# Linear attention followed by a normalised two-layer block: row statistics without bn_stats, more transposes by DMA, and a new order of the same work

## The chip, the cores and the metric

The kernel runs on one core of a Trainium2 chip. A core has five engines with a queue each: TensorE (PE: matmuls, and weight loads shown as PEld), VectorE (DVE), ScalarE (ACT), GpSimd (POOL) and SyncE (SP), which here only issues transfers. Sixteen DMA engines carry the transfers. The metric is the time of one execution on the device in microseconds (us). The kernel before took 157.92 us (median of 3 runs, 157.91 to 160.95).

## The reference

The inputs are `r`, `k`, `v` (4 batches, 8 heads, 768 time steps, head dimension 48), a decay `w` and a bonus `u` per head and channel. The first half is a linear attention with a decaying state, the second half normalises each row of 384 channels and sends it through 384 to 1536 to 384 with a ReLU:

```python
for t in range(S):
    cur = einsum('bhd,bhe->bhde', u[None] * kt, vt)
    y[:, :, t] = einsum('bhd,bhde->bhe', rt, state + cur)
    state = w[None, :, :, None] * state + einsum('bhd,bhe->bhde', kt, vt)
x = y.transpose(0, 2, 1, 3).reshape(B, S, H * D)
mu, var = mean(x, -1), mean((x - mu) ** 2, -1)
xn = (x - mu) / sqrt(var + 1e-06) * g_ln
out = x + maximum(xn @ w_ch1, 0.0) @ w_ch2
```

Inputs and output are float32. The matmul operands in the kernel are bfloat16.

## The kernel before, in words

**Tiles.** The 768 time steps of a batch are cut into 6 chunks of 128, which makes 24 chunks; chunk i of the attention is tile i (128 rows by 384 channels) of the second half. Tiles are taken through the two-layer block in 18 groups, of one tile at first and at the end and of two in the middle (tiles 8 to 19).

**Steps of a chunk.** LK, LR and LV (lines 315 to 322) load k, r and v of a chunk on SP's queue, 192 KB each; in DRAM a row of a head is 48 floats. SK and SR multiply k and r by powers of the decay into bfloat16 tiles `sck` and `scr`. TR (line 333) turns `scr` and `sck` on TensorE, four transposes each, into PSUM; TC, TCr and TCk copy them to `trs` in SBUF. For the chunks in `K_BY_DMA` (18 to 23) k is turned instead by TKD, a DMA transpose that SP issues (line 475), and TR turns r alone. Q multiplies the two halves of `trs`. AT (line 352) forms the 128 by 128 scores of 8 heads, AM masks them on VectorE into `A`, S (line 383) makes the state's update and the bonus, CC copies the bonus out, ZU and ZD update the state `Z`, VB multiplies v by the bonus on GpSimd, Y (line 425) sums the attention in PSUM and X (line 444) adds VB's part: this is `x`.

**Steps of a tile.** ST and AG (lines 447 to 452) take mean and variance of a row with bn_stats and bn_aggr. XN writes mean minus x in bfloat16 (the sign is in the weights, which SW scales by minus g_ln at the start). RS (line 464) forms one over the standard deviation on GpSimd. LT turns the tile on TensorE, three transposes, and XT copies it to `xT`. UP (line 488) does the first layer, in three steps of 12 matmuls for a group of one tile and six steps of 6 wider matmuls for a pair, each into a PSUM tile of 512 columns (two such buffers, `hp`); RL is the ReLU that empties it into `hT`. DN (line 517) does the second layer in three steps of four matmuls into one PSUM tile `o`. OT multiplies by RS and adds x, STO stores the tile.

**Order.** The order of all this is written out in the string `PLAN`: every entry names a step, a chunk (or group and part) and an engine (v, s, g; "-" where the step has only one). Each engine's queue gets its instructions in the order of PLAN and works through them in that order; semaphores set by the framework make an instruction wait for what it reads and for buffers to come free. `SLOTS` gives the number of buffers of each kind: 10 for the loaded k, r and v, 3 for `sck`, `scr` and `trs`, 2 for `q`. All loads, all stores and all DMA transposes stand in the one queue of SP, in the order of PLAN, and each transfer there also waits for the completion of the one eight places ahead. DU steps are matmuls on a zero tile in the first microseconds.

Of the kernel before, what the change touches and what calls it, by code (L numbers as in the profile page):

```python
# [15 lines left out]
K_BY_DMA = [18, 19, 20, 21, 22, 23]  # L16
SLOTS = {'kf': 10, 'rf': 10, 'vf': 10, 'sck': 3, 'scr': 3, 'vv': 4, 'trs': 3, 'q': 2, 'A': 2, 'cc': 4, 'Z': 3, 'ZS': 2, 'Vb': 3, 'x': 13, 'xn': 3, 'xT': 4, 'hT': 4, 'ot': 3}
PLAN = """
MW,0,v WF,0,- TL,0,s MI,0,g MP,0,v WU,13,- MM,0,g LN,0,s LK,0,- ROWSI,0,s WBM,0,- LV,1,-
LR,0,- FK,0,s CV,1,v FR,0,s SK,0,v LK,1,- SR,0,g LR,1,- SK,1,v DU,18,- TR,0,- UW,0,g  # L20
WL,0,s LK,2,- SR,1,g TCk,0,s LR,2,- TCr,0,s SK,2,g Q,0,v DU,22,- TR,1,- LV,0,- AT,0,-
TCk,1,s SR,2,v LG,0,- LW1,2,- TCr,1,s AMa,0,v CV,0,g UGC,0,s AMb,0,v DU,13,- TR,2,- S,0,-
Q,1,v TC,2,s Y,0,- AT,1,- CC,0,v ZU,0,v LV,2,- AMa,1,v VB,0,g DU,3,- S,1,- SW,7,s
AMb,1,v LW1,1,- SW,8,s IW2,0,g X,0,v SW,6,s DU,13,- AT,2,- Q,2,v Y,1,- CV,2,g ST,0,v
AG,0,v LW1,0,- CC,1,s XN,0,s RS,0,g ZU,1,v SW,5,s SW,3,v DU,16,- LT,0,- VB,1,g XT,0,v
SW,4,s DU,6,- UP,2,- X,1,v S,2,- RL,2,s SW,2,g ST,1,v UP,1,- SW,0,s SW,1,v IW2,2,g
AG,1,v AM,2,v UP,0,- XN,1,s IW2,1,g LK,3,- LT,1,- RL,1,s CC,2,v XT,1,v LR,3,- DU,1,-
Y,2,- RL,0,s VB,2,g ZU,2,v UP,18,- SK,3,v LV,3,- DN,0,- SR,3,v RL,18,s UP,17,- X,2,v
TR,3,- CV,3,g ST,2,v RL,17,s UP,16,- RS,1,g TC,3,v AG,2,v RL,16,s Q,3,v AT,3,- XN,2,v
RS,2,g AM,3,v S,3,- LT,2,- DN,1,- XT,2,s CC,3,s UP,33,- ZU,3,v LK,4,- DN,2,- LV,6,-  # L30
VB,3,g UP,32,- OT,0,v Y,3,- SK,4,v LR,4,- DN,4,- RL,32,v RL,33,s DN,5,- CV,6,s LR,5,-
X,3,v SR,4,v DN,6,- LV,4,- ST,3,v TR,4,- SR,5,g UP,34,- OT,1,v LV,5,- TC,4,s AG,3,v
DN,8,- CV,4,v XN,3,g LK,5,- Q,4,v AT,4,- RL,34,s DN,9,- RS,3,g AM,4,v LK,7,- LT,3,-
S,4,- XT,3,s DN,10,- LK,6,- SK,5,v CC,4,s VB,4,g UP,48,- OT,2,v LR,10,- TR,5,- SK,7,v
UP,49,- SK,6,g ZU,4,v RL,48,s LR,6,- TC,5,v Y,4,- CV,5,s DN,12,- RL,49,v LR,12,- ZD,4,g
AT,5,- X,4,v DN,13,- AM,5,v LR,7,- SR,6,g UP,50,- LV,7,- ST,4,v TR,6,- RL,50,s Q,5,v
SR,7,g Y,5,- AG,4,v STO,1,- TC,6,v S,5,- XN,4,s DN,14,- STO,0,- CC,5,v CV,7,s Q,6,v
VB,5,g LT,4,- LV,11,- AT,6,- XT,4,v S,6,- OT,3,v UP,64,- LV,9,- X,5,v CC,6,s UP,66,-
RS,4,g ST,5,v RL,64,s LR,8,- TR,7,- AM,6,v RL,66,s UP,65,- SR,10,g CV,9,s LK,11,- DN,16,-
AG,5,v RL,65,s TC,7,v RS,5,g Y,6,- LR,9,- XN,5,s DN,17,- ZU,6,v VB,6,g Q,7,v LT,5,-  # L40
LK,8,- DN,18,- XT,5,s AT,7,- X,6,v LK,10,- UP,80,- ST,6,v S,7,- SR,8,v RL,80,s LR,14,-
UP,82,- SK,8,g AM,7,v UP,81,- RL,82,s LK,9,- TR,8,- CC,7,s AG,6,v OT,4,v RL,81,s RS,6,g
Y,7,- LK,14,- TC,8,v XN,6,s DN,20,- VB,7,g CV,11,s ZU,7,v LV,8,- LT,6,- DN,21,- Q,8,v
SR,9,g X,7,v XT,6,s AT,8,- LK,15,- SK,9,v DN,22,- CV,8,s UP,96,- ZD,7,g LV,13,- ST,7,v
AM,8,v TR,9,- RL,96,s SK,10,g STO,2,- S,8,- UP,97,- LR,11,- CC,8,s TC,9,v SR,12,g Y,8,-
OT,5,v RL,97,s TR,10,- STO,4,- Q,9,v AT,9,- VB,8,g LK,12,- TC,10,s AG,7,v UP,98,- ZU,8,v
AM,9,v ZD,8,g S,9,- LV,12,- XN,7,s DN,24,- CC,9,s LT,7,- Q,10,v SK,11,g LR,16,- DN,25,-
ZU,9,v RL,98,s X,8,v AT,10,- XT,7,s LV,15,- DN,26,- ZD,9,g ST,8,v UP,114,- AM,10,v LV,10,-
VB,9,g Y,9,- RL,114,s UP,113,- STO,3,- SR,11,g AG,8,v X,9,v XN,8,s LK,13,- UP,112,- CV,10,s
ST,9,v RS,7,g TR,11,- OT,6,v RL,112,s LR,17,- S,10,- AG,9,v TC,11,v RL,113,s SR,14,g Y,10,-  # L50
DN,28,- CC,10,s LR,15,- SK,13,v CV,12,s XN,9,s VB,10,g LT,8,- AT,11,- ZU,10,v LK,17,- DN,29,-
XT,8,s Q,11,v SK,12,g LT,9,- X,10,v DN,30,- LV,16,- XT,9,s AM,11,v S,11,- UP,130,- RS,8,g
LR,13,- UP,129,- CC,11,v OT,7,v RL,130,s ZD,10,g LK,21,- TR,12,- ST,10,v RL,129,s UP,132,- CV,13,v
VB,11,g TC,12,s SR,15,v LK,19,- UP,131,- RL,132,s Y,11,- STO,6,- SR,13,v AT,12,- RL,131,s LK,16,-
Q,12,v UP,128,- AG,10,v X,11,v XN,10,g S,12,- STO,5,- RL,128,s TR,13,- ST,11,v LK,22,- UP,133,-
CV,15,v SR,16,v SK,15,g DN,32,- TC,13,v RL,133,s LR,22,- DN,33,- AG,11,v AM,12,v XN,11,s Q,13,g
LR,21,- LT,10,- CC,12,s DN,34,- XT,10,s ZU,12,v Y,12,- LV,21,- SK,14,g LT,11,- OT,8,v AT,13,-
S,13,- XT,11,v DN,36,- LR,19,- VB,12,g AM,13,v TR,14,- CV,16,g LR,20,- UP,144,- CC,13,v X,12,v
TC,14,s RS,9,g DN,37,- ZU,13,v LV,14,- RL,144,s ST,12,v ZD,13,g UP,145,- STO,7,- UP,148,- RL,145,s
VB,13,g LV,20,- Q,14,v AT,14,- RL,148,s Y,13,- LK,18,- SK,16,v TR,15,- AG,12,v DN,38,- CV,14,v  # L60
TC,15,v LV,22,- UP,149,- OT,9,v XN,12,s TR,16,- LV,23,- Q,15,v RL,149,s DN,40,- X,13,v SR,19,g
LV,17,- ST,13,v UP,147,- TC,16,s AM,14,v UP,146,- LV,19,- RL,147,s LT,12,- CV,17,g S,14,- AG,13,v
RL,146,s XT,12,v AT,15,- LR,18,- CC,14,v Y,14,- XN,13,s SK,17,v DN,41,- ZU,14,v LR,23,- Q,16,v
LT,13,- DN,42,- VB,14,g AM,15,v XT,13,s LK,20,- S,15,- ZD,14,g UP,163,- OT,10,v STO,8,- UP,162,-
RL,163,s X,14,v SR,18,g DN,44,- SK,18,v SR,17,g UP,160,- ST,14,v STO,9,- AT,16,- RL,162,s CC,15,v
AG,14,v Y,15,- LK,23,- AM,16,v RL,160,s RS,10,g TR,17,- CV,19,s UP,164,- VB,15,g LV,18,- TC,17,v
UP,165,- RL,164,s SR,20,g ZU,15,v DN,45,- Q,17,v XN,14,s STO,10,- ZD,15,g TR,18,- S,16,- X,15,v
TCr,18,s DN,46,- ST,15,v UP,161,- AG,15,v OT,11,v Y,16,- RL,161,s SR,21,v XN,15,g AT,17,- TKD,18,-
CV,20,s LT,14,- CC,16,v DN,48,- XT,14,v RL,165,s VB,16,g LT,15,- DN,49,- XT,15,v Q,18,v RS,11,g
UP,180,- X,16,v STO,11,- ZU,16,v DN,50,- SK,19,g ST,16,v S,17,- TR,19,- OT,12,v UP,176,- RL,180,s  # L70
ZD,16,g AG,16,v CC,17,s DN,52,- AM,17,v VB,17,g UP,178,- RL,176,s TKD,19,- SK,20,g DN,53,- XN,16,v
RL,178,s Y,17,- STO,12,- CV,18,g UP,177,- TCr,19,s AT,18,- CV,21,s Q,19,g TR,20,- RL,177,s X,17,v
UP,181,- AM,18,v DN,54,- RL,181,s SR,22,g UP,179,- OT,13,v TKD,20,- SR,23,g AT,19,- ST,17,v RL,179,s
S,18,- DN,56,- TCr,20,v AG,17,v LT,16,- XN,17,s RS,12,g Y,18,- DN,57,- XT,16,v CC,18,s CV,22,s
ZU,18,v LT,17,- VB,18,g DN,58,- XT,17,v AM,19,v UP,197,- STO,13,- Q,20,g TR,21,- UP,192,- X,18,v
OT,14,v S,19,- AT,20,- RL,197,s SK,22,v DN,60,- TCr,21,s UP,195,- ST,18,v CC,19,s ZU,19,v DN,61,-
VB,19,g STO,14,- AM,20,v Y,19,- RL,195,s ZD,19,g S,20,- DN,62,- X,19,v RL,192,s TR,22,- CV,23,s
Y,20,- OT,15,v SK,21,g UP,194,- ST,19,v CC,20,s UP,193,- TCr,22,v RL,194,s TKD,22,- AG,19,v TR,23,-
VB,20,g RL,193,s UP,196,- AG,18,v XN,18,s TCr,23,v DN,64,- TKD,21,- XN,19,g X,20,v RL,196,s LT,18,-
DN,65,- RS,13,g XT,18,v STO,15,- AT,21,- SK,23,g ZU,20,v LT,19,- DN,66,- XT,19,v AM,21,v ZD,20,g  # L80
UP,212,- UP,209,- RL,212,s Q,21,g OT,16,v Y,21,- UP,208,- RL,209,s AT,22,- S,21,- Q,22,g AM,22,v
DN,68,- CC,21,s UP,213,- VB,21,g ZU,21,v RL,208,s DN,69,- ST,20,v RL,213,s STO,16,- ZD,21,g UP,211,-
AG,20,v S,22,- X,21,v RS,14,g RL,211,s DN,70,- ST,21,v TKD,23,- XN,20,s UP,210,- AG,21,v XN,21,v
RS,15,g LT,20,- Y,22,- OT,17,v AT,23,- CC,22,s XT,20,v RL,210,s DN,72,- VB,22,g ZU,22,v AM,23,v
UP,224,- ZD,22,g STO,17,- DN,73,- RL,224,v Q,23,g LT,21,- DN,74,- UP,225,- OT,18,v UP,226,- XT,21,v
RL,225,s X,22,v DN,76,- ST,22,v UP,241,- DN,77,- RL,241,s AG,22,v RL,226,v XN,22,g Y,23,- DN,78,-
STO,18,- RS,16,g UP,240,- OT,19,v LT,22,- S,23,- RL,240,s DN,80,- XT,22,s DN,81,- CC,23,s VB,23,g
UP,257,- DN,82,- RL,257,s X,23,v STO,19,- UP,256,- OT,20,v UP,242,- ST,23,v DN,84,- AG,23,v RL,242,s
XN,23,g DN,85,- RL,256,s RS,17,g LT,23,- DN,86,- XT,23,v UP,272,- OT,21,v UP,258,- STO,20,- DN,88,-
RL,258,s DN,89,- RL,272,s STO,21,- DN,90,- UP,273,- OT,22,v UP,274,- RL,273,s DN,92,- RL,274,s DN,93,-  # L90
STO,22,- DN,94,- OT,23,v STO,23,-
"""


@with_exitstack
def kernel(
    ctx: ExitStack,
    tc: tile.TileContext,
    r: bass.AP,
# [344 lines left out]
    def X(i, e):  # L444
        nc.vector.tensor_tensor(out=xx(i)[:], in0=psum["y", i][:, :C], in1=Vb(i)[:], op=ALU.add)  # L445
# [137 lines left out]
```

## Time and profile before

| | before |
|---|---|
| median of 3 runs | 157.92 us |
| profiled execution, its own time | 156.55 us |
| its span, first to last instruction | 154.4 us |
| PE busy | 146.4 us, 95% |
| DVE busy | 119.4 us, 77% |
| POOL busy | 95.7 us, 62% |
| ACT busy | 76.2 us, 49% |
| DMA transposes | 6, all of k |
| granted clock of TensorE | 0.996 |

The profiled execution was 1.37 us quicker than the median of the timed runs. Between its span and its own time lie 2.13 us. Busy time of PE is modelled and matmuls overlap, so two neighbouring rows of PE can cover the same time; what a step costs in a full queue is read from where the next one starts. Lines such as L525 are lines of the kernel before.

### The profile page before, as it was taken

Reading aid. Unit: us, or ns where it says so; the run is one execution under the profiler, and the core shown is the slowest. Engines: PE = TensorE matmul, PEld = TensorE weight load, DVE = VectorE, ACT = ScalarE, POOL = GpSimd, SP = SyncE. Lnnn points to the kernel's source line nnn. Section 1 sums busy time; section 2 is a strip of 40 time slices with the busy share of each in tenths; the row PEclk is TensorE's granted clock in tenths of the full one; section 3 lists DMA queues with packets and bytes.
Section 4 is the critical chain, followed back from the end, with each engine's and each line's share of the span. In section 5 each row is a group of like instructions: output and inputs, shape, how many; then the busy total and the mean of one; then the engine's idle time right before and its main releaser. Section 6 shows DMA issues by size and latency. Waiting matters only on the chain.

```text
span 154.4 us, 4697 instructions
## 1 busy us (share of the span) xinstructions
PE 146.4 (95%) x1926; PEld 118.6 (77%) x1926; DVE 119.4 (77%) x242; ACT 76.2 (49%) x149; POOL 95.7 (62%) x135
## 2 busy tenths in 40 slices
PE   7689999999899999999999999999999999999990
PEld 4488788868677887979688878877778778878770
DVE  2256989789998999999999999797797769734211
ACT  4526884434155747657535746356455244143330
POOL 3182665356749499995693698798766968333200
PEclk9999999999999999999999999999999999999998
DMA  4999999999999999989899897132153051102111
GB/s 82 192 182 354 349 200 206 210 177 212 226 200 188 199 255 179 257 170 232 170 243 208 176 261 107 51 89 34 51 87 87 0 89 51 51 20 82 56 56 51
DMA packets 84487, 23.51 MB, mean 152 GB/s; under 512 B 79857, under 2 KB 82930, under 8 KB 84466
## 3 DMA queue, kind: packets, MB, share of 16 engines
q1 hardware_dynamic: 83202, 22.03, 64.5%
q0 software_dynamic: 432, 1.18, 4.2%
q8 instruction: 15, 0.25, 0.7%
q10 hardware_dynamic: 832, 0.00, 0.3%
q14 instruction: 6, 0.05, 0.1%
HBM read 18.88 MB, written 4.72 MB: 153 GB/s over the span
## 4 chain that ended last, share of the span: by engine, by line
PE 73%; DVE 16%; DMA 3%; ACT 2%; issue 2%; SPq 1%; POOL 1%; POOLq 0%; DVEq 0%; ACTq 0%
PE o L525 27%; PE hp L497 26%; PE tr L338 5%; PE at L357 4%; DVE A L367 4%; DMA rf<-in_r_dram 3%; PE tr L482 3%; DVE scr L203 2%; PE y L438 2%; PE s L401 2%; PE y L430 2%; PE o L261 2%; DVE x L445 2%; PE s L388 1%; DVE stats L448 1%
## 5 line engine op out<-in xcount | busy, mean ns | idle before, releaser
L513 ACT ACTIVATE hT<-hp 128x512 bf16<-128x512 f32 x68 | 40.0, 597 | 49.5 <-PE hp L497 48.9
L497 PE MATMUL hp<-xT,w_sb 128*128 128x128 bf16 (+1 forms) x648 | 57.2, 237 | 0.3 <-ACT w_sb L306 0.2
L525 PE MATMUL o<-w_sb,hT 128*128 128x384 bf16 x288 | 57.1, 326 | 0.2 <-DVE hT L515 0.2
L497 PEld LDWEIGHTS <-w_sb 128*128 128x128 bf16 x648 | 49.4, 113 | 4.4 <-ACT w_sb L306 0.4
L525 PEld LDWEIGHTS <-hT 128*128 128x128 bf16 x288 | 25.3, 98 | 11.6 <-DVE hT L515 0.4
L367 DVE TENSOR_TENSOR A<-at,mask 128x1024 bf16<-128x1024 f32 (+1 forms) x26 | 29.1, 1127 | 3.3 <-PE at L357 3.3
L420 POOL TENSOR_TENSOR Vb<-vf,cc 128x384 f32<-128x384 f32 x24 | 21.6, 898 | 12.6 <-ACT cc L198 6.7
L203 POOL TENSOR_TENSOR scr<-rf,Fr 128x384 bf16<-128x384 f32 x16 | 16.2, 1019 | 11.7 <-DMA rf<-in_r_dram 8.2
L535 DVE SCALAR_TENSOR_TENSOR ot<-o,rs,x 128x384 f32<-128x384 f32 x24 | 14.7, 611 | 10.3 <-PE o L525 10.2
L445 DVE TENSOR_TENSOR x<-y,Vb 128x384 f32<-128x384 f32 x24 | 13.1, 547 | 4.2 <-POOL Vb L420 3.1
L203 POOL TENSOR_TENSOR Z<-ZS,WLZ 128x384 bf16<-128x384 f32 x13 | 13.6, 1048 | 2.5 <-DVE ZS L414 2.3
L198 ACT COPY trs<-tr 128x512 bf16<-128x512 bf16 (+1 forms) x13 | 10.0, 782 | 10.5 <-PE tr L338 10.5
L448 DVE BATCH_NORM_STATS2 stats<-x 128x6 f32<-128x384 f32 x24 | 13.3, 554 | 0.4
L203 POOL TENSOR_TENSOR sck<-kf,Fk 128x384 bf16<-128x384 f32 x12 | 12.6, 1046 | 0.3 <-PE s L401 0.3
L469 POOL TENSOR_TENSOR rs<-rs,expo 128x1 f32<-128x1 f32 (+1 forms) x18 | 10.9, 603 | 1.5
L338 PE MATMUL tr<-ident,scr 128*128 128x128 bf16 x96 | 9.7, 227 | 1.9 <-POOL scr L203 1.9
L261 PE MATMUL o<-warm 128*128 128x128 bf16 x105 | 10.3, 269 | 1.0 <-DVE warm L226 1.0
L203 DVE TENSOR_TENSOR sck<-kf,Fk 128x384 bf16<-128x384 f32 x12 | 9.6, 799 | 1.4 <-DMA kf<-in_k_dram 1.4
L203 DVE TENSOR_TENSOR q<-trs 128x512 bf16<-128x512 bf16 x18 | 8.8, 489 | 2.4 <-ACT trs L198 2.4
L261 PEld LDWEIGHTS <-warm 128*128 128x128 bf16 x105 | 8.7, 124 | 2.4 <-issue 1.3
L458 ACT ACTIVATE xn<-x,mv 128x384 bf16<-128x384 f32 x15 | 9.2, 613 | 2.5 <-DVE mv L452 2.5
L357 PE MATMUL at<-trs 48*128 48x128 bf16 x192 | 9.8, 222 | 0.4 <-DVE trs L200 0.3
(66 smaller groups left out, 180.2 us busy)
## 6 DMA issues: line engine op xcount, KB each, us to landing
kf<-in_k_dram SPq DMA_DIRECT2D x24, 192.0 KB, 3.9
vf<-in_v_dram SPq DMA_DIRECT2D x24, 192.0 KB, 4.1
rf<-in_r_dram SPq DMA_DIRECT2D x24, 192.0 KB, 3.9
out_dram<-ot SPq DMA_DIRECT2D x24, 192.0 KB, 2.5
w_f<-in_moe_w_ch_dram SPq DMA_DIRECT2D x3, 768.0 KB, 7.3
w_sb<-in_moe_w_ch_dram POOLq DMA_DIRECT2D x3, 384.0 KB, 6.5
trs<-sck SPq DMA_TRANSPOSE x6, 3.6
u_p<-in_u_dram ACTq DMA_DIRECT2D x2, 0.8 KB, 3.1
```

What stands on the lines that cost most here:

```text
L203: engines[e].tensor_tensor(out=out, in0=in0, in1=in1, op=ALU.mult)
L261: nc.tensor.matmul(out=warm_ps[0][:, :P], lhsT=warm[:], rhs=warm[:], start=True, stop=True)
L338: nc.tensor.transpose(out=t[:, a * HP + q, :], in_=flat[:, q, :], identity=ident[:])
L357: nc.tensor.matmul(out=t[:, par, q, :], lhsT=trs(i)[p0 : p0 + D, 1, q, :], rhs=trs(i)[p0 : p0 + D, 0, q, :], start=True, stop=True,)
L367: nc.vector.tensor_tensor(out=AA(i)[:, a:b].rearrange("p e q t -> p (e q) t"), in0=psum["at", i][:, a:b].rearrange("p e q t -> p (e q) t") ...
L420: nc.gpsimd.tensor_tensor(out=Vb(i)[:].rearrange("p (h d) -> p h d", h=H), in0=vf(i)[:], in1=cc(i)[:].unsqueeze(2).to_broadcast([P, H, D]) ...
L445: nc.vector.tensor_tensor(out=xx(i)[:], in0=psum["y", i][:, :C], in1=Vb(i)[:], op=ALU.add)
L448: nc.vector.bn_stats(out=stats[i % 4][:], in_=xx(i)[:])
L497: nc.tensor.matmul(out=t[:, a * gw : (a + 1) * gw], lhsT=w1_sb[n][kc][:, fb::FB], rhs=xT(g)[:, kc, :gw], start=(kc == 0), stop=(kc == CK - 1),
L513: nc.scalar.activation(out=o, in_=s, func=ACT.Relu)
L525: nc.tensor.matmul(out=psum["o", i][:, :C], lhsT=hT(g)[:, fk, j * P : (j + 1) * P], rhs=w2_sb[d][:, a, :], start=(fk == 0), stop=(fk == FK ...
L535: nc.vector.scalar_tensor_tensor(out=ot(i)[:], in0=psum["o", i][:, :C], scalar=rs[g][:, j : j + 1], in1=xx(i)[:], op0=ALU.mult, op1=ALU.add,)
```

## The change

**Statistics.** ST and AG go. X becomes a scalar_tensor_tensor on VectorE (1.0 times y plus VB's part) with an accumulator output, the row's sum `sm`. XN writes the sum minus 384 times x, so the row that is normalised is 384 times larger, and RS takes that into its constants. A new step SQ, on ScalarE, squares the same expression and gives its row sum through an accumulator output; the squares themselves go to a scratch tile that nothing reads.

**Transposes.** `K_BY_DMA` starts at chunk 6 instead of 18. A new step TRD turns r by DMA for chunks 8 to 23; TR is called for chunks 0 to 7 alone. LTD, which was defined and not called, turns tiles 16 to 23 in place of LT and XT. All are issued by SP.

**Order.** PLAN is another order of the steps, with other engines for some. Counts of the steps whose number or engine differs:

| step | before | after |
|---|---|---|
| TR (TensorE transposes in it) | 24 (168) | 8 (56) |
| LT (transposes in it) | 24 (72) | 16 (48) |
| TKD, TRD, LTD on SP | 6, 0, 0 | 18, 16, 8 |
| TC on v, s | 10, 6 | 4, 0 |
| TCr on v, s; TCk on v, s | 3, 5; 0, 2 | 0, 4; 1, 1 |
| XT on v, s | 14, 10 | 10, 6 |
| ST, AG on v | 24, 24 | 0, 0 |
| SQ on s | 0 | 24 |
| XN on v, s, g | 3, 15, 6 | 2, 20, 2 |
| RL on v, s | 4, 68 | 14, 58 |
| CC on v, s | 8, 16 | 15, 9 |
| CV on v, s, g | 5, 13, 6 | 6, 9, 9 |
| Q on v, g | 18, 6 | 21, 3 |
| SK on v, g | 12, 12 | 11, 13 |
| SR on v, g | 8, 16 | 9, 15 |
| SW on v, s, g | 2, 6, 1 | 2, 5, 2 |
| matmuls in WU and DU | 105 | 103 |

The diff, with the order cut to the stretch around the turning of chunk 20 and to the last tiles:

```diff
-K_BY_DMA = [18, 19, 20, 21, 22, 23]
+K_BY_DMA = [6, 7, 8, 9, 10, 11, 12, 13, 14, 15, 16, 17, 18, 19, 20, 21, 22, 23]
 ...
+Y,18,- AT,19,- OT,14,v TRD,20,- S,19,- UP,193,- AM,19,v VB,18,g LV,20,- DN,60,- SK,20,g RL,193,v
+UP,192,- LK,23,- CC,19,v DN,61,- ZU,19,v VB,19,g RL,192,s STO,14,- UP,194,- STO,13,- CV,22,g X,18,v
+UP,195,- SK,22,g STO,12,- RL,194,s TKD,20,- Y,19,- SQ,18,s DN,62,- ZD,19,g X,19,v XN,18,s LV,23,-
+UP,196,- RL,195,s OT,15,v SR,22,g AT,20,- XN,19,s Q,20,v LK,21,- DN,64,- SQ,19,s AM,20,v UP,197,-
 ...
+RS,16,g CC,23,v DN,84,- RL,241,s LTD,22,- VB,23,g Y,23,- RL,242,s DN,85,- X,23,v STO,20,- UP,256,-
+XN,23,s DN,86,- RL,256,v UP,257,- SQ,23,s OT,21,v UP,258,- RS,17,g LTD,23,- RL,257,v DN,88,- DN,89,-
+STO,21,- RL,258,s UP,272,- DN,90,- RL,272,s UP,273,- OT,22,v UP,274,- RL,273,v DN,92,- RL,274,s DN,93,-
 ...
-    stats = [const.tile([P, nc.vector.BN_STATS_DIM], FP32, name=f"stats{a}") for a in range(4)]
-    mv = [const.tile([P, GROUPS[g], nc.vector.BN_AGGR_DIM], FP32, name=f"mv{g}") for g in range(len(GROUPS))]
+    sm = [const.tile([P, 1], FP32, name=f"sm{i}") for i in range(NT)]
+    sq = [const.tile([P, GROUPS[g]], FP32, name=f"sq{g}") for g in range(len(GROUPS))]
+    sqj = const.tile([P, C], BF16, name="sqj")
 ...
     def X(i, e):
-        nc.vector.tensor_tensor(out=xx(i)[:], in0=psum["y", i][:, :C], in1=Vb(i)[:], op=ALU.add)
-
-    def ST(i, e):
-        nc.vector.bn_stats(out=stats[i % 4][:], in_=xx(i)[:])
-
-    def AG(i, e):
+        nc.vector.scalar_tensor_tensor(
+            out=xx(i)[:], in0=psum["y", i][:, :C], scalar=1.0, in1=Vb(i)[:], op0=ALU.mult, op1=ALU.add,
+            accum_out=sm[i][:],
+        )
+
+    def SQ(i, e):
         g, j, _ = group_of[i]
-        nc.vector.bn_aggr(out=mv[g][:, j, :], in_=stats[i % 4][:])
+        nc.scalar.activation(
+            out=sqj[:], in_=xx(i)[:], func=ACT.Square, bias=sm[i][:], scale=-float(C), accum_out=sq[g][:, j : j + 1]
+        )
 
     def XN(i, e):
-        g, j, _ = group_of[i]
-        mean = mv[g][:, j, 0:1]
         if e == "s":
-            nc.scalar.activation(out=xn(i)[:], in_=xx(i)[:], func=ACT.Identity, bias=mean, scale=-1.0)
+            nc.scalar.activation(out=xn(i)[:], in_=xx(i)[:], func=ACT.Identity, bias=sm[i][:], scale=-float(C))
         else:
             engines[e].tensor_scalar(
-                out=xn(i)[:], in0=xx(i)[:], scalar1=-1.0, scalar2=mean, op0=ALU.mult, op1=ALU.add
+                out=xn(i)[:], in0=xx(i)[:], scalar1=-float(C), scalar2=sm[i][:], op0=ALU.mult, op1=ALU.add
             )
 
     def RS(g, e):
         n = GROUPS[g]
         nc.gpsimd.tensor_scalar(
-            out=rs[g][:], in0=mv[g][:, :, 1], scalar1=1e-6, scalar2=1.0, op0=ALU.add, op1=ALU.mult
+            out=rs[g][:], in0=sq[g][:], scalar1=1.0 / C, scalar2=1e-6 * C * C, op0=ALU.mult, op1=ALU.add
         )
 ...
+    def TRD(i, e):
+        flat = scr(i)[:].rearrange("p h d -> p (h d)")
+        nc.sync.dma_start_transpose(out=trs(i)[:, 0], in_=flat)
```

## The prediction

> **What bounds the kernel now.** I read the page's busy times and slices first, then the chain of waits, then busy time by stage, then the lines of the DMA transposes.
>
> ```profile
> span 154.4 us, 4697 instructions
> ...
> PE 146.4 (95%) x1926; PEld 118.6 (77%) x1926; DVE 119.4 (77%) x242; ACT 76.2 (49%) x149; POOL 95.7 (62%) x135
> ...
> PE   7689999999899999999999999999999999999990
> ...
> DMA  4999999999999999989899897132153051102111
> ```
>
> Two rows of the slices are full: PE from about 15 us to the end, the DMA engines from 4 to about 96 us. PE is what the end waits for; this is the chain of waits, whose columns are start, length and what.
>
> ```profile
> 118.35 0.22 PE tr L338 x4
> 118.58 0.66 PE hp L497 x6
> 119.23 0.65 PE o L525 x4
> 119.88 0.17 PE tr L482 x3
> 120.05 0.65 PE o L525 x4
> 120.70 0.33 PE at L357 x8
> ...
> 148.93 1.96 PE o L525 x12
> 150.89 0.03 DVEq L535
> ```
>
> The pieces follow each other without a hole, so this view prices a step in a full queue: four transposes 0.225 us, three 0.165, UP 0.66, DN 0.65, AT 0.33; from the same view Y 0.37 and S 0.27. From AT of chunk 23 (129.72 in this chain) to PE's end at 150.9 are 21.2 us, and the steps that PLAN has there add up to 21.0. The prices hold.
>
> Busy time by stage (us, then PE, PEld, DVE, ACT, POOL with instructions, clock, DMA share, GB/s):
>
> ```profile
> 34.00:64.00 30.00, 29.44 (x462) 23.48 (x460) 28.11 (x51) 15.82 (x34) 23.16 (x29) 1.00 1.01 213
> ...
> 94.00:130.00 36.00, 36.00 (x437) 29.15 (x436) 28.95 (x60) 18.33 (x38) 27.88 (x36) 1.00 0.29 54
> ```
>
> In the early stage DMA is as full as PE; late it is 0.29 busy, and there stand all six transposes of before. A load of 196,608 bytes at some 205 GB/s is about 1.0 us of the 16 DMA engines.
>
> **The change part by part.** All sums are against the profiled execution, 156.55 us, which is 1.37 under the median.
>
> *TensorE loses work.* k of chunks 6 to 17: 12 x 0.225 = 2.7 us. r of chunks 8 to 23: 16 x 0.225 = 3.6. Tiles 16 to 23: 8 x 0.165 = 1.3. Two zero matmuls: 0.1. In all 7.7 us of 135.5; 127.8 stay. All of it is on the path if PE stays full: 156.55 - 7.7 = 148.85, the floor.
>
> *The DMA engines gain work.* 36 more transposes: 12 of k, 16 of r, 8 of rows (three quarters the size). What one costs SP:
>
> ```profile
> L477 SPq DMA_TRANSPOSE trs<-sck x6: 1190/1212/1947, 92.3 to 123.8; - x6
> ...
> DMA to landing us min/median/max: 2.4/3.6/4.3
> ```
>
> 1.2 us of SP's queue (a load needs 0.43 where nothing presses) and 2.4 to 4.3 us to landing. What one costs the DMA engines (call it X) I take from the trace's packet records: 512 packets of 256 bytes each, 27.5 ns on average, over 16 engines: **0.88 us**. The six are not alike: 0.63, 0.63 and 0.79 where little else ran, 1.0 to 1.2 in three that met a 16 KB instruction fetch. In those a few packets lasted 1.1 to 1.8 us instead of 18 ns, and all of them were spread over 1.8 to 2.4 us instead of 0.8: one engine held back held others. These are idle-stage rows; none of before stands in a full DMA queue, so the bounds are 0.63 and 1.19, and I take the mean, 0.88: a fetch (15 in the span) will meet a transpose more often, not less, when there are 42.
>
> *The sum at chunk 20*, where DMA work ahead and PE work behind are largest together. Ahead of TKD 20 and with it SP's order has 67 loads, 15 stores, 6 weight loads, 28 turns of k and r and 2 of rows. From the packet records a load is 0.995 us, a store 0.53, weights 2.24 and 2.17, the rest of each transfer 0.03. Starting at 2.5 us: 2.5 + 66.7 + 7.9 + 13.2 + 3.1 = 93.4, plus 28 X + 2 x 0.75 X = 29.5 X. The same sum for before, up to k of chunk 23, gives 94.2; the last load's packets of the trace end at 93.9. From AT 20 on PE has 19 UP, 24 DN, 4 AT, 4 S, 4 Y: 12.5 + 15.6 + 1.3 + 0.9 + 1.5 = 31.8. After PE's end come 3.45 us of span and 2.13 outside. With 1.0 us from the last packet to AT:
>
> time = 93.4 + 29.5 X + 1.0 + 31.8 + 5.6 = 131.8 + 29.5 X
>
> X = 0.88 gives 157.8, X = 0.63 gives 150.4, X = 1.19 gives 166.9. It breaks even at 0.84. Chunks 12 to 20 are within 1.5 us of each other by this sum, so it does not hang on one chunk. In before the same point was never near: TKD 20 needed only a DMA queue that had been empty for 10 us.
>
> *New waits.* TKD and TRD wait in SP's queue for SK and SR; behind them stand loads and stores. Where DMA is the later one these are early (SK 12 needs S 9, three chunks back), so I add nothing; a blocked SP costs nothing until the transfers under way, up to eight, are used up. AT waits on PE for the landing, UP and DN of older tiles stand behind it: that is the sum above. Q waits on VectorE, with RL (14 there instead of 4), X and OT behind it; it waits for the same landing as AT, so it is late with it, not after it.
>
> *VectorE.* Off: bn_stats 13.3, bn_aggr 4.1, TC 6 x 0.678 = 4.1, TCr 1.2, XT 1.4, SK and XN 1.4. On: RL 10 x 0.676 = 6.8, Q 1.4, CC, CV, SR and TCk 2.6, X from 547 to 611 ns (OT's row, the same operation without an accumulator) 1.5. Net 119.4 - 25.5 + 12.3 = 106.2 us. The accumulator's price is in no row: bounds 0 and one more small instruction, 0.17 (bn_aggr); I take 0, 24 of the upper are 4.1 us. Cover: VectorE then has some 40 us idle. From X to XN a tile loses 0.73 us of statistics; the chain has 1 us of bn_stats in all, so I count nothing.
>
> *ScalarE.* On: SQ 24 x 0.613 (XN's row, same shape) = 14.7, XN 3.1. Off: TC 6.1, TCr and TCk 1.2, RL 6.0, XT 1.9, CC 1.1, CV 2.0, SW 0.7. Net 76.2 - 1.2 = 75.0. SQ's bounds: 0.48 (the shortest row of 128x384 on ACT) and 0.78 (XN and a small copy of 0.163). Cover: ACT waited 48.9 us for hp. Without it a square in front of a ReLU costs up to its length; two hp buffers and the DN between cover one.
>
> *GpSimd.* Off: Q 3.5, SR 1.0, XN 2.3; on: CV 1.7, SK 1.0, SW 0.7. Nothing.
>
> *The end.* From Y 23 to UP 272 PE has DN, UP, DN, UP, UP, DN, DN: 4.6 us. Beside it: X 0.61, XN 0.61, LTD 2.4 to 4.3: 3.6 to 5.5. 0 to 0.9 us; I take 0, nearer the middle.
>
> [...] The clean transpose moved 131,072 bytes in 0.63 us of DMA time, 208 GB/s. [...]
>
> **Rivals.** *PE stays full: 148.85*, 150.2 timed. For it: PE is the bound now and loses 7.7 us. Against: it needs X under 0.58, below every row. *Transposes at their clean cost: 150.4*, 151.8 timed; X from 0.58 to 0.72. For it: three of six rows. Against: those ran beside nothing. *The transposes hold each other back: slower.* One late DMA engine holds the others in every transpose of the full stretch, X = 1.19 as in the first, which met a fetch and stores: 166.9, 168.3 timed; it is slower by over 2% from X = 0.94. For it: the long packets. *The change doesn't do what it says* (VectorE's relief shortens the path): PE waits for VectorE little, so at most the 1 us of bn_stats in the chain.
>
> **How the numbers follow.** Forecast, X = 0.73 to 0.94: 157.8 + 1.4 = **159.2 us** timed, chance 0.34. Clean transposes 0.23, PE full 0.05, held back 0.38 (spread from 161 to 170, so no single time in it is as likely as the forecast). 2% (3.16 us) is about what a measurement tells from no change: 154.8 to 161.1. Faster 0.30, the same 0.33, slower 0.37. The range leaves out the floor and the upper end beyond X = 1.15: 151.5 to 167.5.
>
> **What would show it.** DMA's row stays full to about 120 us instead of 96; PE has holes before AT from chunk 8 on, ended by a transpose; PE work of L357, L497 and L525 unchanged; VectorE near 106 us, ACT near 75. The forecast is wrong if the transposes' packets average under 20 ns or over 32, or if SP, not DMA, is what the transposes queue for (its issues up to TKD 20 are 30 x 1.2 + 67 x 0.43 + others = 75 us of 115, so I don't expect it).

## The result, and the profile after

The changed kernel took **170.09 us** (median of 4 runs, 168.60 to 171.83) against 158.01 us for the kernel before on the same chip: ratio **1.0736**, 95% interval 1.0646 to 1.0825, slower. The forecast was 159.2 us with a range to 167.5. The profiled execution took 168.60 us with a span of 166.5. Line numbers of it are two less than before up to the DMA transposes (L477 is now L475), and two more from LT on (L525 is now L527, L535 is L537).

From the page of the changed kernel: busy time, then the slices of PE, of PE's granted clock and of the DMA engines.

```profile
span 166.5 us, 4501 instructions
...
PE 142.5 (86%) x1788; PEld 111.2 (67%) x1788; DVE 110.4 (66%) x226; ACT 76.1 (46%) x168; POOL 91.5 (55%) x132
...
PE   7958989989999667878929997996995999999990
...
PEclk9999999999999999999995999999999699999999
DMA  4999999999997798999878999899699754452211
```

PE has less work, 1,788 instructions against 1,926, and takes longer over it. Its row is full up to slice 13, some 54 us, has holes from there to 128 us, and is full again to the end. The DMA row stays at 6 to 9 up to slice 32, 133 us.

Where PE waited, by what ended the wait (microseconds in total, times, longest):

```profile
PE o L527 <- DVE ot L537: 5.7, 4, 3.2
PE at L355 <- DMA trs<-sck: 4.2, 4, 1.8
PE at L355 <- DMA trs<-scr: 1.3, 2, 0.7
```

Holes of over 0.25 us in PE's records after the first 30 us add up to 15.1 us, against 0.3 before. Half of the named waits are for the turning itself. The others are for VectorE's OT; what VectorE waited for, from the same view:

```profile
DVE ot L537 <- DMA out_dram<-ot: 6.6, 4, 3.3
...
DVE q L201 <- DMA trs<-sck: 5.2, 4, 3.2
...
DVE q L201 <- DMA trs<-scr: 3.0, 2, 1.7
```

Q waits for landings, and OT for the store of the tile three before it, which must leave the `ot` buffer first. The longest of these makes PE's longest hole, here in the timeline (start, length, what, idle time and releaser):

```profile
81.50 0.57 SPq L544 DMA_DIRECT2D out_dram<-ot  x1
...
85.64 0.62 DVE L537 SCALAR_TENSOR_TENSOR ot<-o,rs,x 128x384 f32<-128x384 f32 x1 [3.25 <-DMA out_dram<-ot]
86.31 0.48 PE L527 MATMUL o<-w_sb,hT 128*128 128x384 bf16 x2 [3.19 <-DVE ot L537]
```

The store is that of tile 5, whose OT was done at 59.1 us; SP came to it at 81.5, right behind two transposes. OT of tile 8 waits for its landing, and PE's next DN for the PSUM buffer that OT of tile 8 frees. So the late queue reaches PE by two ways: AT's inputs and the stores.

The transposes themselves, first line those of k, then those of r, each with time to landing:

```profile
L475 SPq DMA_TRANSPOSE trs<-sck x18: 1191/1342/2499, 40.0 to 143.6; - x18
...
DMA to landing us min/median/max: 2.4/3.7/5.4
L479 SPq DMA_TRANSPOSE trs<-scr x16: 1189/1212/2159, 52.2 to 142.3; - x16
...
DMA to landing us min/median/max: 2.4/3.1/4.4
```

In the packet records of the trace their 256-byte packets average 21.6 ns, 0.69 us of the 16 engines per transpose of k or r. That is under the 0.88 of the forecast. What was not cheap is the queue they stand in. SP's timeline (start, length, what), early in the stretch:

```profile
48.30 1.20 SPq L314 DMA_DIRECT2D kf<-in_k_dram  x1
49.62 2.50 SPq L475 DMA_TRANSPOSE trs<-sck  x1
52.22 2.51 SPq L479 DMA_TRANSPOSE trs<-scr  x2
54.79 0.57 SPq L317 DMA_DIRECT2D rf<-in_r_dram  x1
55.41 0.57 SPq L544 DMA_DIRECT2D out_dram<-ot  x1
56.08 1.21 SPq L475 DMA_TRANSPOSE trs<-sck  x1
57.33 0.58 SPq L317 DMA_DIRECT2D rf<-in_r_dram  x1
57.96 1.78 SPq L320 DMA_DIRECT2D vf<-in_v_dram  x1
```

Each begins where the last one ends. From 40 to 124 us only one gap between two of SP's records is longer than 0.12 us, and it is 0.45, so the records leave SP next to no time in which it waits. All 42 transposes took 59.9 us of its time, 1.43 each. Chunk 20, the one of the forecast's sum, shows what that does. SP issues the key turn of chunk 6 at 40.0 us. From there to that of chunk 20 stand 82 transfers, that first one included, and SP is at them all the time: 29 transposes x 1.48 + 53 plain x 0.65 + 82 gaps x 0.08 = 84 us. So chunk 20's turn is issued at 123.8, and AT of chunk 20 on PE waits for it:

```profile
123.80 1.66 SPq L475 DMA_TRANSPOSE trs<-sck  x1
```

```profile
127.98 0.40 PE L355 MATMUL at<-trs 48*128 48x128 bf16 x8 [1.78 <-DMA trs<-sck]
128.31 1.30 PE L527 MATMUL o<-w_sb,hT 128*128 128x384 bf16 x4
```

From 127.98 the rest follows the forecast's working: 31.8 us of PE work, 1.7 for a stretch at half clock (told at the end), 0.8 of small gaps, 4.2 to the end of the span and 2.1 outside: 168.6.

### The profile page after: what moved, and what is told of

Read it like the earlier page. It is cut to its first block, busy times and chain, and to the rows that moved or that the text cites. A ratio compares the mean times of both kernels' runs of the same rounds, so it can differ in the third digit from the quotient of the medians.

```text
span 166.5 us, 4501 instructions
## 1 busy us (share of the span) xinstructions
PE 142.5 (86%) x1788; PEld 111.2 (67%) x1788; DVE 110.4 (66%) x226; ACT 76.1 (46%) x168; POOL 91.5 (55%) x132
## 4 chain that ended last, share of the span: by engine, by line
PE 41%; DMA 21%; DVE 11%; SPq 10%; POOL 6%; issue 5%; ACT 3%; ACTq 1%; POOLq 0%; DVEq 0%
PE o L527 18%; PE hp L499 15%; DMA trs<-sck 6%; DMA rf<-in_r_dram 5%; SPq L475 3%; DMA trs<-scr 3%; PE at L355 3%; SPq L320 2%; DMA vf<-in_v_dram 2%; DMA w_p<-in_w_dram 2%; POOL Z L201 2%; DVE A L365 2%; DVE x L443 1%; DMA kf<-in_k_dram 1%; POOL Vb L418 1%
## 5 line engine op out<-in xcount | busy, mean ns | idle before, releaser
L527 PE MATMUL o<-w_sb,hT 128*128 128x384 bf16 x288 | 59.5, 334 | 6.3 <-DVE ot L537 5.7
L499 PE MATMUL hp<-xT,w_sb 128*128 128x128 bf16 (+1 forms) x648 | 58.4, 240 | 2.0 <-DVE xT L198 1.1
L515 ACT ACTIVATE hT<-hp 128x512 bf16<-128x512 f32 x58 | 34.1, 594 | 48.6 <-PE hp L499 48.3
L527 PEld LDWEIGHTS <-hT 128*128 128x128 bf16 x288 | 25.9, 99 | 19.2 <-issue 7.8
L537 DVE SCALAR_TENSOR_TENSOR ot<-o,rs,x 128x384 f32<-128x384 f32 x24 | 14.8, 615 | 17.5 <-PE o L527 9.3
L201 POOL TENSOR_TENSOR scr<-rf,Fr 128x384 bf16<-128x384 f32 x15 | 15.7, 1050 | 8.8 <-DMA rf<-in_r_dram 7.5
L201 DVE TENSOR_TENSOR q<-trs 128x512 bf16<-128x512 bf16 x21 | 11.9, 568 | 10.6 <-DMA trs<-sck 5.2
L456 ACT ACTIVATE xn<-x,sm 128x384 bf16<-128x384 f32 x20 | 12.2, 612 | 12.1 <-DVE x L443 12.0
L443 DVE SCALAR_TENSOR_TENSOR x<-y,Vb 128x384 f32<-128x384 f32 x24 | 13.2, 551 | 6.3 <-PE y L436 4.1
L450 ACT ACTIVATE sqj<-x,sm 128x384 bf16<-128x384 f32 x24 | 14.6, 608 | 1.5 <-DVE x L443 1.5
L355 PEld LDWEIGHTS <-trs 48*128 48x128 bf16 x192 | 5.6, 94 | 13.3 <-DMA trs<-sck 5.7
L517 DVE TENSOR_SCALAR hT<-hp 128x512 bf16<-128x512 f32 x14 | 9.6, 687 | 2.2 <-PE hp L499 2.0
L436 PE MATMUL y<-vv,A 128*128 128x48 bf16 x192 | 8.7, 183 | 0.6 <-DVE A L365 0.6
```

The lines of the kernel that those rows point to most:

```text
L201: engines[e].tensor_tensor(out=out, in0=in0, in1=in1, op=ALU.mult)
L355: nc.tensor.matmul(out=t[:, par, q, :], lhsT=trs(i)[p0 : p0 + D, 1, q, :], rhs=trs(i)[p0 : p0 + D, 0, q, :], start=True, stop=True,)
L443: nc.vector.scalar_tensor_tensor(out=xx(i)[:], in0=psum["y", i][:, :C], scalar=1.0, in1=Vb(i)[:], op0=ALU.mult, op1=ALU.add, accum_out=sm[ ...
L450: nc.scalar.activation(out=sqj[:], in_=xx(i)[:], func=ACT.Square, bias=sm[i][:], scale=-float(C), accum_out=sq[g][:, j : j + 1])
L456: nc.scalar.activation(out=xn(i)[:], in_=xx(i)[:], func=ACT.Identity, bias=sm[i][:], scale=-float(C))
L499: nc.tensor.matmul(out=t[:, a * gw : (a + 1) * gw], lhsT=w1_sb[n][kc][:, fb::FB], rhs=xT(g)[:, kc, :gw], start=(kc == 0), stop=(kc == CK - 1),
```

## Experiments

The theories: (T) the transposes cause the loss, through the DMA engines or through SP's issuing, or (O) the new order, the accumulators and the squares do. Medians are set beside the kernel before as it ran on the same chip, 158.8 to 159.1 us in each set.

**All transposes left out.**

```diff
-PLAN with 18 TKD, 16 TRD, 8 LTD
+PLAN without them, all else in place
```

> The changed kernel without its 42 DMA transposes: the steps TKD, TRD and LTD are left out, so chunks 6 and later work on old contents of trs and tiles 16 and later on old contents of xT; order, engines and statistics are those of the changed kernel. If the transposes cause the loss (in whichever resource), PE is full again: 150 to 153 us. If the new order, the accumulators or the squares cause it, it stays above 160.

151.47 us, ratio 0.954 (0.948 to 0.961). The transposes cause the whole loss, and 18.6 us between this and the changed kernel are theirs: 0.44 us for each of 42, where one of k or r on TensorE costs 0.225 of PE. Order and statistics together are not to blame: they leave the kernel 1.3 us over the forecast's floor of 150.2 timed, gains and losses set against each other.

**Half the bytes of the loads; v loads issued by ScalarE; both.**

```diff
-        nc.sync.dma_start(out=vf(i)[:], in_=chunk_src(v, i))
+        n = H if i < 10 else HP                                        # half_loads: also in LK, LR
+        (nc.scalar if i >= 8 else nc.sync).dma_start(out=vf(i)[:, :n], in_=chunk_src(v, i)[:, :n])   # v_on_act: the engine
```

> The changed kernel with loads of k, r and v from chunk 10 on that bring 4 of the 8 heads (the other half of a buffer keeps old data); as many transfers on SP, but 42 x 0.5 = 21 us less work for the DMA engines, 18 of it ahead of the turning of chunk 20. If the DMA engines are the bound, 152 to 158 us. If SP's issuing is the bound at a cost per transfer, 165 to 171.

> The changed kernel with the v loads of chunks 8 to 23 issued by ScalarE instead of SP; the DMA work is the same. If SP's issuing is the bound, 16 loads of some 0.65 us leave its queue, 10 us, and the time falls to 158 to 163. If the DMA engines are the bound, it stays at 167 to 172.

> Both edits on the changed kernel at once: loads from chunk 10 on bring 4 of 8 heads, and the v loads from chunk 8 on are issued by ScalarE. If SP's issuing and the DMA engines hold each other up and nothing else does, relieving both brings it to 152 to 156 us, near the 151.5 without any transposes. If the latency of a transpose to its reader is a cause of its own, it stays at 158 to 161.

| kernel | us | ratio to before (95%) |
|---|---|---|
| changed kernel | 170.09 (168.60 to 171.83) | 1.074 (1.065 to 1.083) |
| v_on_act | 165.85 (162.51 to 168.12) | 1.045 (1.035 to 1.054) |
| half_loads | 160.96 (159.33 to 165.73) | 1.013 (1.007 to 1.019) |
| half_loads_v_on_act | 156.82 | 0.988 (0.982 to 0.993) |
| no_turns | 151.47 | 0.954 (0.948 to 0.961) |

Both single edits missed both theories' numbers and fall between them: 4 us from v on ScalarE (2 to 8 by the single runs), 9 from half the bytes, 13 together. The two together missed as well, but by less: 156.82 where the first theory said 152 to 156. Busy time by stage for 60 to 120 us (length, PE, PEld, DVE, ACT, POOL, clock, DMA share, GB/s), the changed kernel, then half_loads:

```profile
60.00:120.00 60.00, 49.80 (x595) 38.61 (x595) 39.67 (x81) 32.31 (x75) 33.23 (x43) 0.97 0.97 171
```

```profile
60.00:120.00 60.00, 52.59 (x641) 41.92 (x638) 43.25 (x86) 34.50 (x79) 38.54 (x50) 1.00 0.72 141
```

With half the bytes DMA is 0.72 busy and PE is still without work for 7 us of 60: something else is the bound, and SP is still issuing 55 of the 60 us from 40 to 100. So relieving DMA helped mostly by making SP's issues shorter. From the first transpose to that of k of chunk 20 stand the same 82 transfers, and SP idles in neither run; they took it 76.4 us instead of 83.8 (a plain one 0.57 instead of 0.65, a transpose 1.36 instead of 1.48). That is 7.4 of the 9.1 us. Why an issue took longer where the DMA engines were fuller (0.97 against 0.72) is not shown.

**Plain copies in the transposes' places.**

```diff
-        nc.sync.dma_start_transpose(out=trs(i)[:, 1], in_=flat)
+        nc.sync.dma_start(out=trs(i)[:, 1], in_=flat.rearrange("p (q t) -> p q t", q=HP))   # TRD, LTD alike
```

> The changed kernel with each of the 42 DMA transposes replaced by a plain DMA copy between the same tiles, without turning: same places in SP's queue, same waits before and after, but 128 rows of 1 KB instead of 512 packets. If the loss is the throughput of SP and DMA on transposes, it falls to within 4 us of the 151.5 without any: 152 to 155. If it is one more trip through SP's queue and a DMA's latency in front of AT, whatever the trip carries, it stays at 160 and more.

153.58 us, ratio 0.970 (0.963 to 0.977): 16.5 of the 18.6 us are gone though 42 transfers still stand in the same places with the same waits. The same stretch as above (DMA share and GB/s at the end), and the copies of k:

```profile
60.00:120.00 60.00, 58.54 (x712) 46.18 (x707) 47.37 (x95) 36.91 (x85) 42.18 (x55) 1.00 0.88 210
```

```profile
L475 SPq DMA_DIRECT2D trs<-sck x18: 471/691/2540, 42.4 to 127.2; - x18
```

A trip through SP and a landing (median 3.4 us for k here) in front of AT are not the loss; what the transfer costs while it passes is.

**SP's time alone, and DMA work alone, on top of the copies.**

```diff
+    def more(i, half):                       # copies_more_sp: behind each copy of k and r
+        for a in range(2):
+            nc.sync.dma_start(out=tiny[:, o : o + 16], in_=ident[:1, :16])
```

```diff
-    trs = ring("trs", [P, 2, HP, P], BF16)
+    trs_wide = ring("trs", [P, 2, HP, P + 16], BF16)     # copies_more_dma
+    trs = lambda i: trs_wide(i)[:, :, :, :P]
```

> The kernel with plain copies in place of the transposes (153.6 us, output not turned), with two tiny transfers of 32 bytes into a scratch row issued by SP behind each copy of k and r: 68 more entries in SP's queue, some 0.45 us each, 1 us per copy, and next to no DMA work; they also use two of the eight transfers under way. If SP's time is what the transposes cost, 34 us more of it bring back most of the loss: 160 to 167. If DMA work is, it stays at 153 to 156.

> The kernel with plain copies in place of the transposes, the buffers of trs widened by 16 columns so that each copy is cut into 512 packets of 256 bytes, as a transpose is, instead of 128 of 1 KB; one transfer per copy as before, so SP issues as many. DMA work goes from 0.39 to some 0.6 us per copy, 7 us in all. If DMA work is what the transposes cost, 157 to 161; if SP's time is, 153 to 155.

copies_more_dma: 156.10 us (154.03 to 157.67, too spread for a ratio), 2.5 us over the copies, between the two numbers expected. Its packets of 256 bytes took 18.1 ns; DMA work grew by 6.4 us in all. copies_more_sp: **185.09 us**, 31.5 over the copies, ratio 1.166 (1.156 to 1.176), beyond what either theory said. In its timeline the pairs of tiny transfers cost 1.23 us each time:

```profile
71.64 0.58 SPq L552 DMA_DIRECT2D out_dram<-ot  x1
72.27 0.43 SPq L315 DMA_DIRECT2D kf<-in_k_dram  x1
72.81 0.69 SPq L481 DMA_DIRECT2D trs<-sck  x1
73.54 1.24 SPq L477 DMA_DIRECT2D tiny<-ident  x2
```

and by stage the DMA engines are far from full while PE has 16 us of holes in 60:

```profile
60.00:120.00 60.00, 44.18 (x482) 32.58 (x482) 33.03 (x66) 26.53 (x62) 27.60 (x34) 0.89 0.61 148
```

34 x 1.23 = 42 us more of SP's time cost 31.5 us with no DMA work to speak of; some 7 of these are 13.7 us at half clock. SP's time by itself is enough to produce a loss of this kind and size: the transposes have 60 us of it where the copies have some 32. Each transfer also waits for the one eight places ahead, and the tiny ones take such places, but this was not what SP waited for. Of 100 transfers from 40 to 124 us whose landing the trace gives, none began less than 1.1 us after the one eight places ahead had landed, and in the changed kernel none less than 3.3 us.

The profiled runs fit this. The time at which SP issues the turn, or copy, of k of chunk 20 tells the time of the execution to within 3 us:

| profiled run | chunk 20 issued at | execution | difference |
|---|---|---|---|
| copies_more_sp | 138.9 | 183.5 | 44.6 |
| changed kernel | 123.8 | 168.6 | 44.8 |
| v_on_act | 118.4 | 162.5 | 44.1 |
| half_loads | 116.6 | 159.3 | 42.7 |
| half_loads_v_on_act | 115.1 | 156.9 | 41.8 |
| copies_more_dma | 112.9 | 155.8 | 42.9 |
| copies | 111.1 | 154.1 | 43.0 |

What stays open is how much of SP's longer time is the DMA engines' doing. The transposes do more to these than their own packets: beside them a load's packet averages 16.9 ns against 15.7 with copies of the same packet size, a 4-byte packet 31 against 9 in the same queue, together with the rest some 15 us of DMA time.

**All transposes issued by ScalarE.**

```diff
-        nc.sync.dma_start_transpose(...)
+        nc.scalar.dma_start_transpose(...)      # TKD, TRD, LTD
```

> The changed kernel with all 42 transposes issued by ScalarE instead of SP, in the same places of the order; DMA work unchanged, SP loses 42 x 1.4 = 59 us of issuing, ScalarE gets it and has 131 us then. If SP's issuing is the larger part of the loss and ScalarE can hold it: 158 to 164 us. If the DMA engines are, or if the ReLUs now wait behind the transposes: 167 and more.

182.60 us, ratio 1.145 (1.134 to 1.156), the second expectation in its number. Its trace does not bear out late ReLUs as the reason. PE's longest waits are again for the turned k and r, and it waits 1.0 us for a ReLU of ScalarE:

```profile
PE at L355 <- DMA trs<-sck: 8.4, 4, 2.7
PE at L355 <- DMA trs<-scr: 6.3, 4, 2.4
```

So the turns come later still from ScalarE's queue, in which they stand among its own work; what holds them there was not tried.

**Fewer transposes.**

```diff
-TRD,i,-  (chunks 8 to 23)      LTD,i,-  (tiles 16 to 23)
+TR,i,- TCr,i,v                 LT,i,- XT,i,v                 # k_only, on the changed kernel
-TR,i,-  TCr,i,e                                              # late_turns, on the kernel before,
+TRD,i,-                                                      # chunks 18 to 23
```

> The changed kernel with r from chunk 8 and rows from tile 16 turned on TensorE again (TR and TCr in the place of TRD, LT and XT in the place of LTD, the copies on VectorE); k from chunk 6 stays with the DMA, 18 transposes. PE gets 4.9 us back. If the number of transposes is what overloads SP and DMA, 24 fewer leave both under PE: 155 to 158 us. If any transpose in the full stretch costs a landing that PE waits for, over 162.

> The kernel before with one addition: r of chunks 18 to 23 is turned by the DMA too (TRD in the place of TR, no TCr), in the stretch where DMA is 0.29 busy and SP waits; PE loses 6 x 0.225 = 1.35 us of work. If the transposes are harmless where SP and DMA are free, 0.5 to 1.4 us faster than before (ratio 0.991 to 0.997). If a transpose costs PE a wait wherever it stands, slower than before by 1 to 3 us.

k_only: 163.95 us, ratio 1.032 (1.024 to 1.039). That is the number of the second expectation (over 162), but not its cause: in the profiled run no wait of PE is for a tile turned by DMA. Its largest are 2.1 us in four waits for VectorE's copies out of PSUM and 1.8 us for a ReLU. Over no_turns plus 4.9 us of PE the time is 7.6 us longer, 0.42 for each of 18 transposes, but the edit also puts 24 copies out of PSUM back on VectorE, so 0.42 is not shown as the price of a transpose here. late_turns: 162.41 us, ratio 1.020 (1.013 to 1.027): even six more, late, where DMA is 0.29 busy, cost about 3 us instead of saving 1.35, as the second expectation had it. The profiled run is the slowest of the six (164.42). Between AT of chunks 17 and 23 it has 35.7 us where before has 31.9. Most of that is one place. SP's timeline, and PE's longest wait:

```profile
119.10 2.28 SPq L462 DMA_TRANSPOSE trs<-scr  x1
121.48 1.21 SPq L458 DMA_TRANSPOSE trs<-sck  x1
122.87 1.19 SPq L462 DMA_TRANSPOSE trs<-scr  x1
124.11 1.26 SPq L458 DMA_TRANSPOSE trs<-sck  x1
```

```profile
PE at L338 <- DMA trs<-sck: 2.5, 1, 2.5
```

Four transposes in a row fill SP for 6 us; the last, k of chunk 21, is the one that PE needs next. PE waits 2.5 us and then runs 3.4 us at half clock. SK of chunk 21 was done on GpSimd at 120.1, and the transpose of 124.11 begins 0.05 us after the one ahead of it, so the queue set the 124.11. Ahead of the four SP had itself stood still, 3.0 us for the OT of a store and 2.0 for another wait: what held it there was the order, not the work.

**The statistics alone, on the kernel before.**

```diff
-X as tensor_tensor; ST,i,v ; AG,i,v
+X with accum_out;   SQ,i,s in AG's place (stats_only) or behind XN (stats_late)
```

> The kernel before with the change of the statistics alone: X with the accumulator, SQ on ScalarE in the place of AG, no ST and AG; transposes and the rest of the order as before. If the transposes cause the loss: 156.5 to 158.5 us, no difference. If the statistics cause a part of it: over 160.

> The kernel before with the change of the statistics, SQ behind XN on ScalarE instead of in front of it. With SQ in front it was 1% slower than before. If that was the 0.61 us of SQ in front of XN, the 0.73 us of bn_stats and bn_aggr now leave the way from x to xn and it is level or better: ratio 0.990 to 1.002. If the accumulators or the fuller ScalarE queue cost it, 1.005 to 1.015 again.

160.45 us, ratio 1.010 (1.004 to 1.015), and 160.07 us, ratio 1.012 (1.005 to 1.018), the second expectation both times. So the statistics cost about 1% by themselves and the place of SQ is not why. ScalarE grows from 76.2 to 88.9 us there, since the copies that the changed kernel takes from it are still on it. Which of its instructions PE then waits for was not tried.

**Without DMA transposes at all (two runs that don't answer the question).**

```diff
-TR,i,- TCr,i,e TKD,i,-  (chunks 18 to 23)
+TR,i,- TC,i,e in TKD's place          # pe_turns; stats_late_pe with the statistics
```

> The kernel before without DMA transposes: k of chunks 18 to 23 is turned on TensorE too, 6 x 0.225 = 1.35 us more for PE. The 42 transposes of the changed kernel cost 18.6 us over leaving them out, 0.44 each, and the 18 of k 7.5, 0.42 each. If one costs that here too, 6 x (0.43 - 0.225) = 1.2 us faster than before (ratio 0.992). If the six of before are hidden, 1.35 us slower (1.009).

> Both edits on the kernel before: statistics with SQ behind XN, no DMA transposes. The sum of the two, 0.985 to 0.995 if each does what its theory says; over 1.005 if neither does.

164.43 and 163.81 us, ratios 1.038 and 1.039. In both, TR of chunk 18 stands behind SR of chunk 21, which shares its buffer, so chunk 18 is worked on with chunk 21's r, and every turn stands right in front of its AT. They say nothing of what the six transposes of before are worth.

## Why the prediction was wrong

*PE is what the end waits for, and it loses 7.7 us.* Right. With the transposes left out the time is 151.47 against 150.2 by that step.

*X, the DMA time of a transpose: 0.88, bounds 0.63 to 1.19.* Inside the bounds, but high: 0.69. With it the forecast's own sum gives 131.8 + 29.5 x 0.69 = 152.2, and the profiled run took 168.6. So the sum failed, not X.

*"If SP, not DMA, is what the transposes queue for ... 75 us of 115, so I don't expect it."* This is the step that failed. It set SP's time against the whole 115 us. But SP's order puts the first transpose at place 35 of 143, and SP got there at 40.0 us (the 35th transfer of before began at 41.1). Only the rest counts: 82 transfers in the 74 us up to DMA's 113.8 (93.4 + 29.5 x 0.69). Even at the prices of the trace of before (1.2, 0.43, 0.05 between) they need 62 us, so SP was nearly full beside the DMA engines; at the prices they had (1.48, 0.65, 0.08), 84, of which it waited next to nothing. I took minimum prices although the same trace had 0.85 us for a plain transfer with DMA full. That a blocked SP costs nothing was argued from inputs that are early; SP needed no late input to be late, and the stores behind the transposes, which hold OT, were in no step of mine. So the wait that the sum left out is that for SP itself.

*The rival in which transposes hold each other back, 168.3 timed.* Right in time, and slower was given the largest chance, but its mechanism is a part at most: the 256-byte packets averaged 21.6 ns, and the long ones it was built on are few, 40 of 20,480 over 0.5 us. Most of the loss returned with next to no DMA work when SP's time was raised: 31.5 us over the copies in copies_more_sp, at a DMA share of 0.61 from 60 to 120 us.

*PE has holes before AT from chunk 8 on, DMA full to about 120 us.* Both happened, so neither told the theories apart: a DMA share of 0.97 at 171 GB/s is not the same as full, the copies moved 210 GB/s at 0.88.

*VectorE 106 us, ScalarE 75.* 110.4 and 76.1. The accumulators were left at 0, and that was nearly right. Here the accumulator was a second instruction on both engines, 84 ns on VectorE and 188 on ScalarE; it is the second line of each pair:

```profile
L443 DVE SCALAR_TENSOR_TENSOR x<-y,Vb x24: 544/549/559, 14.2 to 153.1; 128x384 f32<-128x384 f32 x24
L443 DVE DVE_READ_ACCUMULATOR x<-y,Vb x24: 76/84/85, 14.7 to 153.6; 128x1 f32 x24
```

```profile
L450 ACT ACTIVATE sqj<-x,sm x24: 598/606/636, 14.8 to 154.3; 128x384 bf16<-128x384 f32 x24
L450 ACT ACTIVATION_READ_ACCUMULATOR sqj<-x,sm x24: 185/188/209, 15.3 to 154.8; 128x1 f32 x24
```

In the records the second instruction begins before the first has ended, by 74 ns on VectorE and 99 on ScalarE. X with its read takes 0.56 us where X alone took 0.55, and X itself did not get longer (549 against 547 ns), where the sum had 611. SQ with its read takes 0.70 us, inside the bounds. VectorE's surplus is in other rows: Q took 568 ns each time instead of 489, 1.7 us in all, and the copies of v (CV) 691 instead of 373, 1.9 in all. Why these got longer is not shown.

*Readings that do not come out.* Redone in the same way with X = 0.88, the sum gives 152.5 to 158.5 for chunks 12 to 20, not times within 1.5 us of each other; chunk 20 is still the latest. Three of the six weight loads stand in GpSimd's queue and not in SP's, which changes nothing in a sum of DMA work. The transpose of 0.79 us had company too: it met the end of a 16 KB fetch (104.2 to 105.3 us).

*The end: rows by DMA cost nothing.* Right: no hole of over 0.25 us stands after 128 us.

*A transpose against a copy.* Packets of 256 bytes took 18.1 ns on average as a copy (copies_more_dma), 18 median and 21.6 mean as a transpose. SP's time differed more: 1.2 us at least to issue a transpose, 0.47 for the copy of k.

## What to carry to other kernels

Here a transfer had three prices: the DMA engines' time (0.69 us for a transpose of k or r), its landing (3.7 us median for k, 3.1 for r), and its time in the queue that issues it (1.48 us for a transpose, 0.65 for a plain transfer, from the first turn to that of chunk 20), where it stood in order with all other transfers of SP. Work the third as a sum from the place where the queue really gets to, with prices from a stage as full as the new one will be: a plain transfer priced at 0.43 took 0.65. Here a transpose of k or r saved 0.225 us of the busiest engine, and a transpose cost 0.44 us of the end.

## What the hardware showed that I had not expected

**TensorE's granted clock was 0.5 after some short holes.** In the changed kernel the granted clock is 0.5 from 87.5 to 91.0 us and from 128.5 to 131.9, 3.4 us each, just after holes of 3.2 and 1.8 us; a DN step then takes up to 1.3 us instead of 0.65. By half of 3.4 us, an estimate, each cost some 1.7 us beyond its hole. What sets it off is not shown, and it is not the length of a hole alone: in copies_more_sp two holes of 3.0 and 2.9 us (from 92.3 and 123.3 us) were followed by no slow stretch, and one of 1.8 (from 108.2) was.

**A 32-byte transfer took as much of SP's time as one of 192 KB.** The tiny ones of copies_more_sp took 0.62 us each, the loads of 192 KB from 40 us on 0.63.

**Moving v's issue to another engine helped by 4 us with the same loads.** v_on_act took 165.85 us against 170.09. SP came to the turn of k of chunk 20 at 118.4 us instead of 123.8, with the DMA engines just as full (1.00 from 60 to 120 us, 0.97 in the changed kernel): issue time was what was short.
